# Local attention on 32-row tiles with values loaded two keys to a partition, in a fused attention and token-mixing kernel

## The chip, the core and the metric

The kernel runs on one core of one Trainium2 chip. The metric is the device time of one execution in microseconds (us), quoted as the median of the runs. Two engines' names are used all the time: PE is the matmul engine (PEld its weight loads), DVE the vector engine; ACT, POOL and SP are the scalar, the general and the DMA-issuing engine. A "batch" is one of the 8 entries of the leading axis; the kernel is software-pipelined over them. Its period is read from the start of the matmuls into the tile `pwd` (the projection of the pooled tokens, "hyper-weights" in the prediction), one group of four per batch, to that of the next batch.

## The reference, cut to what matters

```python
B, H, S, D = 8, 8, 576, 64           # q, k, v: float32 [B, H, S, D]
# attention, per batch and head
q_d, k_d, v_d = (mean over groups of 4 tokens)             # 144 tokens
out_up    = repeat(softmax(scale * q_d @ k_d.T) @ v_d, 4)  # pooled part
mask      = abs(i - j) < 4                                 # local window
out_local = softmax(where(mask, scale * q @ k.T, -1e9)) @ v
x = (out_up + out_local) as [B, S, H * D]                  # 576 x 512
# token mixer, per batch; w_q, w_k: 512 x 64, w_out: 512 x 512
W_tok = (x @ w_q) @ (x @ w_k).T / 8
out   = relu(W_tok @ x) @ w_out                            # float32
```

The local part needs only a narrow band of keys for each query. The mixer is computed as M2 = (x @ w_k).T @ x first, then (x @ w_q) @ M2.

## The kernel before

Queries are cut into ten windows of 56 to 58; each needs 64 keys. Scores are computed with the keys on the partitions of the result, two windows and two heads at a time on four 64x64 tiles of the PE array. The names `psc`, `pav`, `pm`, `po` and `pol` of the profile are the result tiles of scores, values, M2, output and last rows of the output.

```python
WQ = [58, 58, 58, 58, 56]            # queries of a window; two windows per n
PAIRS = [(0, 3), (1, 2), (4,)]
# ...
def load_v(b):                       # 64 keys of a window on 64 partitions, 256 B runs
    v32 = st[b]["v32"] = big.tile([128, NW, H, D], FP32, name="v32", tag="v32")
    for n in range(NW):
        for c in range(2):
            sp.dma_start(v32[64 * c:64 * c + 64, n],
                         _ap(v[b], K0[2 * n + c] * D, [[D, 64], [S * D, H], [1, D]]))
# ... scores: 80 matmuls a batch
for i, n in enumerate(pr_):
    for hl in range(NP):
        for p, c in ((0, 0), (1, 1), (0, 1), (1, 0)):
            m = 2 * n + c
            o = i * W + hl * w
            pe.matmul(p_[64 * c:64 * c + 64, p, o:o + w],
                      kT[64 * p:64 * p + 64, hl, K0[m]:K0[m] + 64],
                      qT[64 * p:64 * p + 64, hl, Q0[m]:Q0[m] + w],
                      start=False, stop=True, skip_group_check=True,
                      tile_position=(64 * p, 64 * c))
# ... values: 80 matmuls a batch, on the two diagonal tiles only
for s_ in range(2):
    for hh in range(NP):
        for c in range(2):
            h = 4 * (s_ ^ c) + hh
            pe.matmul(p_[64 * c:64 * c + 64, h // 4, 65 * hh:65 * hh + 65],
                      E[64 * c:64 * c + 64, h % 2, i, h // 2, :],
                      v16[64 * c:64 * c + 64, n, h, :],
                      start=True, stop=True, tile_position=(64 * c, 64 * c))
# ... M2: 7 matmuls of 512 columns
pe.matmul(p_, w_[NW][0:112], g["od"][0][0:112], start=True, stop=False)
pe.matmul(p_, w_[NW + 1], g["od"][1], start=False, stop=False)
for n in range(NW):
    pe.matmul(p_, w_[n], x[n], start=False, stop=(n == NW - 1))
# ... last 64 rows of the output: a group of its own in each batch
for r in range(4):
    pe.matmul(p_, rmx[:, r * S + 512:r * S + 640], wo16[:, r, :],
              start=(r == 0), stop=(r == 3))
# ... a fixed order of the stages (batch offset, stage), repeated for each batch
ORDER = [(-2, "og1"), (-1, "wtd"), (0, "sums"), (1, "cast_qk"), (-1, "wt"), ...]
```

The softmax here doesn't subtract the row's maximum and nothing guards it: scores larger than these inputs give would overflow.

## Time and profile before

| | before |
|---|---|
| median of 3 runs | 193.96 us (193.18 to 194.33) |
| span of the profiled execution | 192.7 us |
| PE busy, whole span | 155.5 us (81%) |
| period of a batch | 19.3 us, PE busy 18.52 of it |
| DMA packets | 74,027, of them 52,432 under 512 B |
| PE instructions (matmuls and weight loads; the trace lists 5,440) | 5,442 |

These are lines of the profile's page of the kernel before. The first three divide the span into slices: busy share of PE in tenths, granted clock of PE in tenths of full speed, busy share of the DMA engines. The two queue lines are packets, MB, and share of the 16 engines' time. The last is the chain of work that ended last, by engine.

```profile
PE   0034448885899989998999899989998999898790
PEclk9999555999789999999999999999999999999997
DMA  5999999899899799967999899969996943004215
...
q1 hardware_dynamic: 73920, 40.12, 81.7%
q8 instruction: 21, 0.34, 0.7%
...
PE 68%; DVE 17%; ACT 7%; issue 4%; POOL 2%; ACTq 0%; DVEq 0%
```

PE is full from slice 13 on; the DMA engines are nearly as full.

The table of windows of the kernel before, two of its periods. After the length come the busy times of PE, PEld, DVE, ACT and POOL with instruction counts, then granted clock, DMA share and GB/s.

```profile
62.00:81.30 19.30, 18.52 (x342) 12.43 (x340) 12.32 (x29) 13.22 (x17) 13.59 (x13) 1.00 0.93 244
81.30:100.60 19.30, 18.52 (x342) 12.44 (x340) 12.32 (x29) 13.17 (x17) 13.58 (x13) 1.00 0.87 234
```

PE works 96% of a period, at full clock; no other engine passes 14 us. PE is the bound of the steady state.

The timeline of PE in the kernel before (start, length, group, idle time before it and what ended it):

```profile
44.17 0.38 PE L27 MATMUL pm_847<-od_0_210,wk_206 128*128 128x512 f16 x1
44.39 0.38 PE L27 MATMUL pm_847<-x_424,wk_206 128*128 128x512 f16 x1
...
45.97 0.23 PE L27 MATMUL pav<-v_1_149,E_1_143 64*64 64x65 f16 x3
48.52 0.38 PE L27 MATMUL pav<-v_1_149,E_1_143 64*64 64x65 f16 x13 [2.33 <-issue]
...
103.00 0.45 PE L27 MATMUL psc<-qT,kT 64*64 64x58 f16 x32
104.69 0.45 PE L27 MATMUL pav<-v_1_149,E_0_131 64*64 64x65 f16 x16
```

M2's matmuls start about 215 ns apart. 32 score matmuls take 0.45 us, and only 16 value matmuls take the same; they use two tiles of four. At 45.97 PE stops in the middle of a group of 16 like matmuls, and the profile knows no wait for it: "issue".

### The profile page before, as it was taken

What the parts mean: (1) busy time and instruction counts of PE and PEld (TensorE: products, weight loads), DVE (VectorE), ACT (ScalarE), POOL (GpSimd) and SP (SyncE); (2) the same over time, 40 slices, a digit from 0 to 9 for tenths busy, and PEclk for the clock granted to TensorE, in tenths of its full rate; (3) what the DMA queues carried; (4) which work ended last, traced back from release to release, by engine and by line L of the source; (5) the groups of instructions that cost most, each with busy time, mean ns of one, the idle gap of its engine ahead of it and who ended that gap; (6) DMA issues with size and microseconds to landing.
All of it is one profiled execution on the core that took longest, in us unless ns stands there. A gap on an engine that the chain in (4) does not pass through costs nothing.

```text
span 192.7 us, 6374 instructions
## 1 busy us (share of the span) xinstructions
PE 155.5 (81%) x2720; PEld 104.0 (54%) x2720; DVE 114.8 (60%) x286; ACT 110.7 (57%) x140; POOL 107.7 (56%) x122
## 2 busy tenths in 40 slices
PE   0034448885899989998999899989998999898790
PEld 0034227853576647664776476647764776465330
DVE  6263978754646566656665666566656665685220
ACT  2037134954565767576757675767576757633422
POOL 5701991099748991895479547954895476000000
PEclk9999555999789999999999999999999999999997
DMA  5999999899899799967999899969996943004215
GB/s 175 314 187 215 348 290 162 191 354 175 175 319 218 174 264 294 263 137 201 278 323 156 184 280 346 187 154 296 330 215 154 300 146 112 3 3 153 93 57 188
DMA packets 74027, 40.54 MB, mean 210 GB/s; under 512 B 52432, under 2 KB 68880, under 8 KB 74000
## 3 DMA queue, kind: packets, MB, share of 16 engines
q1 hardware_dynamic: 73920, 40.12, 81.7%
q8 instruction: 21, 0.34, 0.7%
q14 instruction: 6, 0.05, 0.1%
q10 hardware_dynamic: 80, 0.03, 0.1%
HBM read 30.67 MB, written 9.44 MB: 208 GB/s over the span
## 4 chain that ended last, share of the span: by engine, by line
PE 68%; DVE 17%; ACT 7%; issue 4%; POOL 2%; ACTq 0%; DVEq 0%
PE po L27 15%; PE psc L27 6%; PE pav L27 5%; PE pw L27 4%; PE px L27 4%; PE pca L27 4%; PE pol L27 4%; DVE kd_127 L27 3%; PE pv L27 2%; PE pcs L27 2%; ACT kT L27 2%; PE pod L27 2%; DVE rz L27 1%; PE pws L27 1%; PE pwd L27 1%
## 5 line engine op out<-in xcount | busy, mean ns | idle before, releaser
L27 ACT COPY os<-po 128x1024 f32<-128x1024 f32 x16 | 16.2, 1012 | 14.7 <-issue 8.3
L27 DVE RECIPROCAL rz<-pav 128x8 f32<-128x8 f32 x40 | 8.1, 204 | 13.4 <-PE pav L27 13.4
L27 PE MATMUL po<-wo_91,rmx_227 128*128 128x512 f16 x64 | 15.3, 379 | 0.6 <-ACT rmx_227 L27 0.6
L27 PE MATMUL po<-wo_91,rmx_212 128*128 128x512 f16 x64 | 15.1, 379 | 0.0
L27 DVE COPY xT<-px 128x928 f16<-128x928 f16 (+1 forms) x32 | 13.8, 451 | 0.6
L27 PE MATMUL pq_236<-id_67,q_229 128*128 128x128 f16 x16 | 1.9, 312 | 12.6 <-DVE q_229 L27 12.6
L27 PE MATMUL psc<-id_67,neg 64*128 64x232 f16 (+1 forms) x80 | 9.4, 278 | 2.8 <-DVE vblk_201 L27 2.8
L27 PEld LDWEIGHTS <-rmx_227 128*128 128x128 f16 x80 | 7.2, 98 | 8.1 <-ACT rmx_227 L27 0.7
L27 PE MATMUL psc<-qT,kT 64*64 64x58 f16 (+1 forms) x640 | 11.4, 198 | 0.0
L27 PEld LDWEIGHTS <-rmx_212 128*128 128x128 f16 x80 | 7.2, 98 | 6.6
L27 DVE RECIPROCAL rc<-pca 128x8 f32<-128x8 f32 (+1 forms) x16 | 3.4, 211 | 11.8 <-PE pca L27 11.8
L27 PEld LDWEIGHTS <-wqk_90 128*128 128x128 f16 x96 | 8.3, 98 | 3.7 <-issue 0.9
L27 PEld LDWEIGHTS <-kT 64*64 64x64 f16 x640 | 8.7, 113 | 2.1 <-issue 2.1
L27 ACT COPY odT<-pod 128x448 f16<-128x448 f16 (+1 forms) x16 | 5.6, 402 | 6.3 <-PE pod L27 6.3
L27 PE MATMUL pw<-xT,wqk_90 128*128 128x288 f16 x64 | 9.2, 286 | 0.0
L27 PEld LDWEIGHTS <-q_229 128*128 128x128 f16 x16 | 1.6, 146 | 12.6 <-DVE q_229 L27 12.6
L27 POOL CAST v_0_147<-v_79 128x2560 f16<-128x2560 f32 x1 | 3.1, 3129 | 9.3 <-DMA w_92<-in_moe_w_k_dram 9.3
L27 DVE TENSOR_TENSOR wT_219<-pw,wTd 128x576 f16<-128x576 f32 x4 | 3.0, 758 | 8.6 <-ACT wTd L27 8.6
L27 DVE COPY ol<-pol 64x512 f32<-64x512 f32 x8 | 5.5, 682 | 4.3 <-PE pol L27 4.3
L27 DVE TENSOR_TENSOR wT_204<-pw,wTd 128x576 f16<-128x576 f32 x4 | 3.0, 758 | 8.0 <-ACT wTd L27 6.6
L27 DVE TENSOR_SCALAR rmx_227<-pmx 128x1024 f16<-128x1024 f32 x4 | 4.9, 1224 | 4.1 <-PE pmx L27 4.1
L27 POOL CAST v_1_149<-v_255 128x2560 f16<-128x2560 f32 x1 | 2.3, 2323 | 8.6 <-DMA v_255<-in_v_dram 8.6
(542 smaller groups left out, 540.9 us busy)
## 6 DMA issues: line engine op xcount, KB each, us to landing
out_dram<-os SPq DMA_DIRECT2D x16, 512.0 KB, 4.4
v_79<-in_v_dram SPq DMA_DIRECT2D x10, 128.0 KB, 4.6
v_255<-in_v_dram SPq DMA_DIRECT2D x10, 128.0 KB, 5.4
v_583<-in_v_dram SPq DMA_DIRECT2D x10, 128.0 KB, 3.5
v_1024<-in_v_dram SPq DMA_DIRECT2D x10, 128.0 KB, 4.4
v_1497<-in_v_dram SPq DMA_DIRECT2D x10, 128.0 KB, 3.6
v_1970<-in_v_dram SPq DMA_DIRECT2D x10, 128.0 KB, 4.3
v_2443<-in_v_dram SPq DMA_DIRECT2D x10, 128.0 KB, 3.4
```

The source lines that it names most:

```text
L27: return lambda *a, **k: self._tc.keep_in_program_order(f_(*a, **k))
```

## The change

The intent: fewer, larger DMA packets and less PE time. Values are loaded two keys to a partition, in 512 B runs. A window's 64 keys then lie on 32 partitions in two planes (even and odd keys), so scores and values run on 64x32 and 32x64 tiles, twice as many matmuls. M2 is split into two halves of 256 columns on two column tiles that are to run side by side. The remainders of q and k (the last 64 tokens) are loaded by head in 1 KB runs. The last rows of two batches share one output group. Outputs go out in 4 KB runs. The first batches get a hand-made order, and constants are set later. The core of the diff:

```diff
-PAIRS = [(0, 3), (1, 2), (4,)]
+NT = 3
 ...
-            for c in range(2):
-                sp.dma_start(v32[64 * c:64 * c + 64, n],
-                                  _ap(v[b], K0[2 * n + c] * D, [[D, 64], [S * D, H], [1, D]]))
+            for m in (2 * i, 2 * i + 1):
+                for s_ in range(1 if n < 2 else 2):
+                    c, nh = (m % 4) ^ (3 * s_), H if n < 2 else 4
+                    sp.dma_start(t[32 * c:32 * c + 32, 8 * n:8 * n + nh],
+                                 _ap(v[b], 4 * s_ * S * D + K0[m] * D, [[2 * D, 32], [S * D, nh], [1, 2 * D]]))
 ... (scores: 80 matmuls become 160)
+                for f in range(2):
+                    for hl in range(nh):
+                        for c in range(4):
+                            for p in range(2):
+                                ...
+                                pe.matmul(p_[32 * c:32 * c + 32, p, o:o + w],
+                                          _ap(kT, 64 * p * row(kT) + S * hh + K0[m] + f, [[row(kT), 64], [2, 32]]),
+                                          qT[64 * p:64 * p + 64, hh, Q0[m]:Q0[m] + w],
+                                          start=False, stop=True, skip_group_check=True,
+                                          tile_position=(64 * p, 32 * c))
 ... (values: 80 matmuls become 160)
+                                pe.matmul(ps_[t_][64 * c2:64 * c2 + 64, s_, 65 * hh:65 * hh + 65],
+                                          E[32 * c:32 * c + 32, hh % 2, f, 2 * a + hh // 2, :],
+                                          v16[32 * c:32 * c + 32, 8 * n + 4 * a + hh, f, :],
+                                          start=(f == 0), stop=(f == 1), skip_group_check=True,
+                                          tile_position=(32 * c, 64 * c2))
 ... (M2)
-            for n in range(NW):
-                pe.matmul(p_, w_[n], x[n], start=False, stop=(n == NW - 1))
+            for i, (*w_, x_) in enumerate(l_):
+                for c in range(2):
+                    pe.matmul(p_[64 * c:64 * c + 64, 0:256], w_[c], x_[:, 256 * c:256 * c + 256], start=(i == 0),
+                              stop=(i == len(l_) - 1), skip_group_check=True, tile_position=(0, 64 * c))
 ... (last rows, every second batch)
+            if b % 2 == 0:
+                return
-                pe.matmul(p_, rmx[:, r * S + 512:r * S + 640], wo16[:, r, :],
+                pe.matmul(p_, rest[b // 2][:, r, :], wo16[:, r, :], start=(r == 0), stop=(r == 3))
 ... (order of the first batches; order of the others; result-buffer slots; constants: cut)
```

The program has 8,770 PE instructions after, 5,442 before: 3,328 more.

## The prediction

> **What bounds it now.** In the table of windows, five consecutive batches between 62 and 158.5 us take 19.3 us each, with PE busy 18.52 (96%), ACT 13.2, POOL 13.6, DVE 12.3 us; the chain of waits is PE almost without a break there. So PE bounds the steady state. DMA is close behind: share 0.81 to 0.93. In the packet records, 50,176 packets of 256 B take 18 ns each (median; 70.8 us of a 16-engine total of about 160), a 1 KB packet 46 ns. The rest: 62 us until the second batch's hyper-weights, with PE idle 12.6 us before its first matmul, 5.2 us for the cast of v, 2.8 us behind DVE adds (7.6 us in the chain), and a clock of 0.75; then a 16.6 us tail after the last hyper-weights.

> **What changes, costed per batch (start-to-start distances of PE in one 19.3 us batch).**
> - m2: 7 matmuls of 512 columns, 1.62 us, become 14 of 256 on two column halves that should run side by side: -0.75. Eight more small transposes: +0.1.
> - Last rows of two batches share one output group: 4 matmuls of 216 ns every second batch: -0.43.
> - Local scores: 80 matmuls of 58 columns on 64x64 tiles become 160 on 64x32 tiles. Neighbours now start 4 ns apart, four in about 32 ns. [...] eight at 4 ns fill the same 32 ns, so about 0 to +0.3.
> - Local values: 80 matmuls of 65 columns, 17.5 ns apart (only two diagonal tiles used), become 160 on eight tiles at 4 to 8 ns: -0.7 to 0.
> - Masks, pooled v and remainders: about the same columns.
> Sum: about -1.6 us of PE per batch. ACT gains the remainder copies and one relu (about 14 us), DVE and POOL stay under 14: PE remains the bound, the period about 17.7 us.
> - DMA: v's 40,960 packets of 256 B become 20,480 of 512 B (27 ns for the few in the trace), remainders 8,192 to 2,048, outputs 4 KB runs: 160 to about 128 us in all. [...] bytes per ns rise from 14 to 19. It matters at the start only.
> - Start: loads and casts in halves, sums of batch 0 on PE (+2 us of PE, -9 us of DVE), constants set later, a hand-made order of the first batches. Two batches' loads need about 25 us. I estimate the second batch's hyper-weights at 48 us instead of 62.
> - Tail: m2 -0.7, two relus in sequence on ACT +0.8: unchanged, 16.5 us.

> **Time.** 48 + 5 x 17.7 + one period without loads 15.9 + 16.5 = 169, plus 1 us by which timed runs exceed the profiled span: **170 us**, 8 in 10 between **162 and 179**. Faster by over 2%: **0.96**; within 2%: **0.03**; slower: **0.01**.

> **What would show each step.** Windows: period 17 to 18.5 us with PE over 93% busy. Timeline: m2's 14 matmuls in about 0.85 us; scores of a 64-matmul group in 0.3 to 0.5 us; value matmuls under 8 ns apart. DMA share of the steady state under 0.9. First transposes near 10 us, second hyper-weights near 48 us. Tail within 1 us of before.

> **What would make it wrong.** 32-row tiles that don't overlap (17 ns apart would add 2 us a batch); 3,300 more PE instructions outrunning instruction fetch, seen as "issue" gaps like the 2.33 us one at 46 us; PSUM slots or ACT order stalling PE; a start bound by DMA or POOL, not by order; slow 32-partition loads.

The sum came to about -1.6 us of PE per batch, so a period of about 17.7 us and 170 us in all. That eight matmuls on eight tiles fill the 32 ns of four was the estimate, from the 4 ns between neighbours on four tiles; no run had shown it.

## The result, and the profile after

| | before | after |
|---|---|---|
| median | 193.6 us (4 runs) | 227.75 us (227.11 to 232.5, 4 runs) |
| ratio of fast runs | 1 | 1.175, 95% interval 1.169 to 1.181 |
| PE busy | 155.5 us | 173.8 us |
| PE at half clock (clock records within the span) | 19.2 us | 51.2 us |
| DMA packets | 74,027 | 45,448 |
| start of the second batch's `pwd` | 62.1 us | 62.1 us |

All ratios in this document are the mean time of one kernel's fast runs over that of the other's of the same rounds, so they are not quite the ratio of the medians. The changed kernel is 17.5% slower, not 12% faster: the prediction missed by 58 us and had given "slower" a chance of 0.01.

The page of the kernel after, the same lines:

```profile
PE   1458687696974599999973999368976799979791
PEclk9999758969799599999999799785997559999999
DMA  5989959979899999045867069920297003200415
...
q1 hardware_dynamic: 45408, 40.12, 62.6%
q8 instruction: 34, 0.56, 1.1%
...
PE 67%; issue 14%; ACT 7%; DVE 4%; DMA 3%; SPq 2%; ACTq 0%; DVEq 0%
```

The data queue q1 did drop from 81.7% to 62.6%. But PE has holes all along its row, the clock row shows half speed behind many of them, and the chain gives 14% of the span to "issue", time for which the profile has no cause. The DMA row has holes too, so it isn't the loads that fill the time.

The windows of the kernel after, same columns as before:

```profile
81.30:100.60 19.30, 19.11 (x517) 13.59 (x515) 11.03 (x29) 13.39 (x18) 13.15 (x9) 1.00 0.53 173
...
120.00:139.20 19.20, 15.58 (x322) 11.02 (x322) 8.76 (x23) 10.81 (x12) 7.86 (x5) 0.91 0.54 145
139.20:158.50 19.30, 12.95 (x407) 9.76 (x395) 7.11 (x18) 8.14 (x13) 7.05 (x6) 0.73 0.51 146
```

No engine and not DMA is full in the second and third line, and the clock is down. The periods are 19.8, 26.3, 21.4, 24.7, 28.0, 27.7 and 18.5 us; before, 19.3 each.

The waits of PE in the kernel after (total us, times, longest):

```profile
PE pav L27 <- issue: 10.5, 5, 3.8
PE pwk L27 <- issue: 7.7, 2, 5.7
PE psc L27 <- issue: 5.9, 4, 2.0
```

The timeline of PE in the kernel after:

```profile
92.69 0.68 PE L27 MATMUL psc<-qT,kT 64*32 64x58 f16 x64
...
94.51 0.71 PE L27 MATMUL pav<-v,E 32*64 32x65 f16 x64
...
99.32 0.71 PE L27 MATMUL pm<-x,wk 128*64 128x256 f16 x10
...
138.77 0.97 PE L27 MATMUL psc<-qT,kT 64*32 64x56 f16 x96
...
140.83 0.21 PE L27 MATMUL pav<-v,E 32*64 32x65 f16 x2
144.81 0.78 PE L27 MATMUL pav<-v,E 32*64 32x65 f16 x62 [3.77 <-issue]
```

The array works nearly as hoped: 64 score matmuls in 0.68 us and 64 value matmuls in 0.71 us, M2's matmuls two at a time. Then PE stops for 3.77 us after the second of 64 like matmuls, for which everything was there. So it isn't data, nor a result buffer.

A listing worked out from the traces (not a view of the profile), for the blocks around three stops of the kernel after and around the one of the kernel before; "runs" is the time between a block's first and last start, and "fetch" is the packet that landed last before the next block's start:

```
        block  starts   runs   fetch                 next block starts  stop
after    9      68.04   2.19      73.46- 74.72              76.16       5.92
after   18     117.87   2.21     121.36-122.37             123.88       3.81
after   21     138.80   2.03     142.44-143.37             144.81       3.97
after   14      97.41   4.23      98.50- 99.60             101.64       0.00
before   2      42.03   3.97      45.65- 46.99              48.52       2.52
before  10     103.17   4.00     103.96-105.07             107.16       0.00
```

The pattern is the same everywhere. The fetch for the next block as a rule begins only once the current block runs (median 1.4 us after its start, in both kernels, but up to 4.3 us before and 5.4 us after; 3 of the 34 after began 0.2 to 1.2 us ahead of it), takes about 1.1 us, and at the stops PE goes on 1.2 to 1.7 us after it has landed. Together about 3.9 us, more where the fetch is late. A block that lasts longer than its own fetch takes, delay included, hides this. Before, the shortest lasts 3.97 us, and that one stopped; two of 4.00 us did not. After, score and value matmuls fill a block in 2.0 to 2.7 us, and PE runs dry; two blocks of 5.6 us stopped as well, by 0.6 and 1.2 us, because their fetches began only 3.8 and 3.9 us after the blocks did.

The stop is then, by bookkeeping, the fetch's delay + its length + the time until PE goes on - the time for which the block runs. For block 21, with its own delay and the usual 1.1 and 1.4 us: 3.64 + 1.1 + 1.4 - 2.03 = 4.1 us, measured 3.97. The test of the pairing is another one. In the traces of all eleven kernels, with the packets paired to the borders in order, there are 276 borders with a packet of their own: at none does PE go on sooner than 1.16 us after its packet has landed, and at the 60 where it stood still for over 0.5 us, it goes on 1.16 to 1.66 us after.

### The profile page after: what moved, and what is told of

Same layout as the page of the kernel before. It is cut to its first block, busy times and chain, and to the rows that moved or that the text cites. A ratio compares the mean times of both kernels' runs of the same rounds, so it can differ in the third digit from the quotient of the medians.

```text
span 226.0 us, 9679 instructions
## 1 busy us (share of the span) xinstructions
PE 173.8 (77%) x4384; PEld 125.4 (55%) x4384; DVE 102.5 (45%) x291; ACT 119.4 (53%) x153; POOL 99.5 (44%) x100
## 2 busy tenths in 40 slices
DMA packets 45448, 40.72 MB, mean 180 GB/s; under 512 B 3424, under 2 KB 42336, under 8 KB 45408
## 3 DMA queue, kind: packets, MB, share of 16 engines
q1 hardware_dynamic: 45408, 40.12, 62.6%
## 4 chain that ended last, share of the span: by engine, by line
PE 67%; issue 14%; ACT 7%; DVE 4%; DMA 3%; SPq 2%; ACTq 0%; DVEq 0%
PE po L27 12%; PE psc L27 8%; PE pav L27 6%; PE pm L27 4%; PE pca L27 4%; PE pq L27 4%; PE pmx L27 4%; PE pv L27 4%; PE px L27 3%; DMA r<-in_k_dram 3%; PE pw L27 3%; PE pk L27 3%; ACT E L27 3%; SPq L27 2%; PE pol L27 2%
## 5 line engine op out<-in xcount | busy, mean ns | idle before, releaser
L27 POOL TENSOR_TENSOR sum<-qT 128x1152 f32<-128x1152 f16 x7 | 14.7, 2105 | 58.0 <-ACT qT L27 58.0
L27 PE MATMUL po<-wo,rmx 128*128 128x512 f16 x128 | 30.2, 380 | 0.3 <-DVE rz L27 0.3
L27 DVE TENSOR_TENSOR x<-pav,rz 128x512 f16<-128x512 f32 x40 | 27.7, 692 | 1.4
L27 PE MATMUL pav<-v,E 32*64 32x65 f16 x1280 | 17.3, 216 | 11.7 <-issue 10.5
L27 ACT ACTIVATE E<-psc 128x928 f16<-128x928 f32 (+1 forms) x24 | 19.3, 812 | 13.2 <-PE psc L27 12.2
L27 ACT COPY qT<-pq 128x2048 f16<-128x2048 f16 (+1 forms) x8 | 14.1, 1759 | 12.9 <-PE pq L27 12.9
L27 ACT ACTIVATE Ec<-pcs 128x576 f16<-128x576 f32 (+1 forms) x16 | 12.2, 771 | 12.3 <-PE pcs L27 11.9
L27 POOL CAST k<-k 128x2048 f16<-128x2048 f32 x7 | 13.2, 1892 | 11.7 <-DMA k<-in_k_dram 6.4
L27 ACT ACTIVATE rmx<-pmx 128x1024 f16<-128x1024 f32 x16 | 16.2, 1022 | 4.0 <-PE pmx L27 3.6
L27 DVE COPY xT<-px 128x464 f16<-128x464 f16 (+2 forms) x40 | 14.2, 394 | 6.9 <-PE px L27 6.4
L27 POOL CAST v<-v 128x2560 f16<-128x2560 f32 x7 | 16.3, 2323 | 2.1 <-DMA r<-in_q_dram 1.7
L27 POOL TENSOR_TENSOR sum<-kT 128x1152 f32<-128x1152 f16 x7 | 14.7, 2105 | 4.7 <-ACT kT L27 4.6
L27 POOL CAST q<-q 128x2048 f16<-128x2048 f32 x7 | 13.2, 1891 | 2.9 <-DMA q<-in_q_dram 2.9
```

The source lines that it names most:

```text
L27: return lambda *a, **k: self._tc.keep_in_program_order(f_(*a, **k))
```

## The experiments

**Theory A**: PE consumes the dense blocks of small matmuls faster than the next 256 instructions arrive; the clock drops after the stops. **Rival B**: the 32-row tiles are slow of themselves, or the new order and result-buffer slots make PE wait, and the position of the stops is chance. **Rival C**: with v in 512 B runs the loads disturb something else, such as q and k arriving late. On one core, a run counts as slow here when it is over 1.5% above the fastest of its kernel. The profiled executions of the first, third, fifth and eighth kernel below were such runs; from those I take positions of stops and lengths of undisturbed periods, and no differences of a few per cent.

### 1. The kernel after without the loads of later batches (wrong)

```diff
 def f_(b):                               # loads of q and k; the same for v
+    if b > 1:
+        st[b]["qk"[i] + "32"] = st[1]["qk"[i] + "32"]
+        return
```

> The changed kernel, but batches 2 to 7 reuse batch 1's q, k and v in the on-chip buffers, so most data loads are gone (results wrong on purpose); the 8,770 tensor-engine instructions are the same. Theory A (the tensor engine outruns its instruction fetch: one 16 KB packet of 256 instructions [...] waits behind data DMA): the packet's start comes within about 1 us of the block's start, as in the quietest blocks of before; stalls at block borders fall from 28 us to under 10 us, the clock recovers, total 180 to 200 us. Rival B (32-row and 32-column tiles are slow by themselves, or the new order stalls): total within 5 us of 227.

Measured: 199.83 us median (197.65 to 203.51), ratio to before 1.025 (1.019 to 1.032). 13 stops remain, 16.5 us in all, all at borders of 256. The page of this run:

```profile
DMA  5989997400100431061204022200220042002225
...
q1 hardware_dynamic: 16416, 19.67, 31.7%
```

With the DMA engines nearly empty after the start, half of the stopped time goes. The long delays of the fetch go with it: from 60 us on, 1 fetch of 25 began over 2 us after its block, the latest 2.1 us; in the kernel after, 9 of 26 did, the latest 5.4 us. The median is 1.1 us in both. So data traffic makes some fetches late, and PE outruns them even without traffic. The expected "under 10 us" of stops was a miss, and the time is at the top of the range. Rival B had expected 222 us or more for this kernel, which has the same small tiles, order and result buffers.

### 2. The kernel before with 160 tiny matmuls more in each batch (correct results)

```diff
+    pe.matmul(p_[64 * c:64 * c + 64, p, 500:504],        # 4 columns nobody reads
+              kT[64 * p:64 * p + 64, hl, K0[m]:K0[m] + 64],
+              qT[64 * p:64 * p + 64, hl, Q0[m]:Q0[m] + 4],
+              start=False, stop=True, skip_group_check=True,
+              tile_position=(64 * p, 64 * c))
 # and the like behind each value matmul
```

> The kernel before, with a second matmul of only 4 columns, into unused columns, after each of the 160 local-attention matmuls of a batch: 8,002 tensor-engine instructions instead of 5,442, still on 64x64 tiles, same order, same data loads. Theory A: stalls of 1 to 4 us at multiples of 256 instructions appear, 10 to 25 us in all, and the clock drops after them; total 215 to 240 us. Rival B (the tiles or the new order are to blame, not the count): only the array time of the added matmuls, at most 2 us a batch, so 200 to 210 us and no stalls at block borders.

Measured: 243.45 us median; one fast run of 234.84, the others up to 248.51, so no interval. 10 stops, 21.1 us, all at borders of 256, and 49.6 us at half clock. Timeline and waits of PE of this run:

```profile
121.41 0.68 PE L27 MATMUL psc<-qT,kT 64*64 64x4 f16 x57
125.83 0.27 PE L27 MATMUL psc<-qT,kT 64*64 64x4 f16 x3 [3.75 <-issue]
```

```profile
PE pav L27 <- issue: 10.9, 5, 3.9
PE psc L27 <- issue: 5.8, 4, 3.8
```

The first two lines have the plainest reading: of the 60 score matmuls that are left of a group, 57 have run, and PE stands still for 3.75 us before the other three. (The view puts the form of the first one on the row; real ones of 58 columns and tiny ones of 4 are mixed in it.) Nothing but instructions was added to the kernel before: same tiles, same order, same loads, same result buffers. It got stops of the same kind, at the same numbers. Such stops therefore need neither B nor C. A's range was 215 to 240 us and the fast run lies in it, but the median lies above. What the added matmuls cost by themselves and what the half clock costs were not separated; in the profiled execution PE's busy time is 26.1 us above that of before and its idle time 13.9 us, so the stops are not all of the loss.

### 3. The kernel after with 64x64 tiles for local attention (wrong by my own mistake)

Scores, values (on two diagonal tiles), masks, pooled v and the loads of v as before; all else as after: 5,938 PE instructions. The halves of the heads were put in the wrong order in x, so the result is wrong. The same work is done.

```diff
-                        for c in range(4):
-                            for p in range(2):
+                        for p, c in ((0, 0), (1, 1), (0, 1), (1, 0)):
 ...                           # one matmul of 64 keys in place of two of 32; same for values
```

> The changed kernel with only the local attention (and with it the loading of v, one key to a partition in 256 B runs) put back to 64x64 tiles; the new order, remainders by head, m2 by halves and shared last rows stay. 5,938 tensor-engine instructions. Theory A: stalls at block borders under 5 us, period about 17.5 to 18.5 us, total 170 to 185 us, so faster than both. Rival C (the new order and start are to blame): stays above 205 us.

Measured: 201.71 us (198.69 to 203.4), ratio 1.033 (1.025 to 1.042). The stops at borders are two, 6.2 us; but 170 to 185 us was expected, so the time was a miss. Two other costs appeared: the loads are in 256 B packets again (q1 share 79.8%, 62.6% in the kernel after), and the chain gives 19% to DMA and 14% to the DMA-issuing queue. Taking the small tiles away removes most of the stops (6.2 us are left of 32.5), but this kernel has another limit.

### 4. The kernel after with the dense stages spread apart (correct results)

```diff
-(-2, "m2"), (-1, "mask1"), (-1, "score1"), (-1, "av2"), ...
+(-2, "m2"), (-1, "mask1"), (-1, "score1"), (-3, "og1"), (-1, "av2"), ...
-(0, "score2"), (1, "load_k"), (0, "score0"), ...
+(0, "score2"), (-2, "og0"), (1, "load_k"), (0, "score0"), ...
 # ol moved ahead of av0, too; the stores one batch later
```

The output matmuls (16 in about 3.8 us, dense in time but not in number) go between scores and values.

> The changed kernel, same instructions, but in the repeated part of the order (batches 5 to 7 only) the long output matmuls stand between the groups of small ones, so that 256 instructions last longer where they are dense. Theory A: the 2 us blocks become 3.5 us or more, total 3 to 10 us less than 227. Rival B: within 1.5 us of 227.

Measured: 224.32 us (223.35 to 230.53), ratio 1.159 (1.153 to 1.164), 3.4 us less than after in the medians, at the low end of what was expected. In the part whose order was changed, from 114 us on, the stops above 0.5 us at borders fall from 18.1 to 4.6 us, and the time at half clock from 27.3 to 1.3 us. The time does not follow. The waits of PE in this kernel from 114 us to the end of the last stores show why:

```profile
PE pod L27 <- DVE od L27: 4.3, 5, 1.1
PE po L27 <- DVE vblk L27: 2.9, 3, 1.0
...
PE pmx L27 <- ACT os L27: 2.1, 4, 0.5
```

PE now waits for DVE and ACT, 9.3 us in these three lines alone. In all, its idle time from there on is 24.5 us, in the kernel after 24.4; its busy time is 82.5 us in place of 87.2, although one group of eight output matmuls more (1.7 us) falls into that part. Going by the names, the moved output matmuls stand before stages whose data or result buffers are not ready yet. So the order governs the stops, as A says, and this order trades them for other waits. Of the half clock it shows that 26 us less of it came with only about 6 us less of busy time. A good order might exist; none was found here.

### 5. The kernel before with what is left of the change (correct results)

M2 in column halves, shared last rows, 4 KB outputs; no small tiles, no new loads, the old order: 5,522 PE instructions.

```diff
-            for n in range(NW):
-                pe.matmul(p_, w_[n], x[n], start=False, stop=(n == NW - 1))
+            for i, (w_, x_) in enumerate(l_):
+                for c in range(2):
+                    pe.matmul(p_[64 * c:64 * c + 64, 0:256], w_, x_[:, 256 * c:256 * c + 256], start=(i == 0),
+                              stop=(i == len(l_) - 1), skip_group_check=True, tile_position=(0, 64 * c))
 ... # ol and the stores as in the changed kernel
```

> The kernel before, in its own order and with its own local attention and loads, plus three parts of the change that add few instructions: m2 by column halves, the last rows of two batches in one output group, outputs in 4 KB runs. 5,522 tensor-engine instructions (before 5,442). If the prediction priced these parts rightly (-0.75 and -0.43 us of the tensor engine per batch) and the steady state is bound by that engine: period 18.1 instead of 19.3 us, total 183 to 187 us, faster than both kernels, no more stalls at block borders than before (one). If data DMA (share 0.81 to 0.93 before) takes over as the bound: 187 to 192.

Measured: 189.69 us (187.54 to 191.07), ratio 0.974 (0.968 to 0.981): faster than both, and than the kernel before by 1.9 to 3.2%, so that 2% is not quite assured. It is within the second of the two ranges expected. One of its undisturbed periods in the windows:

```profile
77.60:96.00 18.40, 17.12 (x345) 12.36 (x344) 11.73 (x28) 13.29 (x18) 12.67 (x12) 1.00 0.90 224
```

The period is 18.4 us, 0.9 less than before (the prices of the prediction gave 1.2). DMA is at 0.90 in it, PE at 93%; that the seventh kernel, with DMA at 0.15 to 0.27, has periods of 18.2 to 18.4 speaks for PE as its bound, but that is another kernel, and no run of this one without loads was made. Two stops at borders, 4.7 us together, made one period 22.5 us and one 20.1: this kernel is close to the fetch as well.

### 6. The fifth kernel and the remainders by head (correct results)

```diff
-            sp.dma_start(r32[64 * i:64 * i + 64],
-                              _ap(src, 512 * D, [[D, 64], [S * D, H], [1, D]]))
+            sp.dma_start(r32[:, i], _ap(src, 512 * D, [[S * D, H], [4 * D, 16], [1, 4 * D]]))
 ... # 16 small matmuls in place of 4 transposes
```

> As e5, and the remainders of q and k loaded by head in 1 KB runs (12 more small matmuls a batch, 192 instructions in all; remainder packets from 8,192 to 2,048). If the tensor engine bounds e5: within 1 us of it. If DMA bounds e5: 1 to 4 us faster.

Measured: 190.99 us (188.66 to 192.6), three of six runs slow, ratio of the fast ones 0.976 (0.970 to 0.983). The two intervals overlap, and the medians of the fast runs are 189.38 us here and 189.42 in the fifth kernel: fewer packets for the remainders gain nothing that these runs can see, which is what was expected if PE is the bound.

### 7. The third kernel mended, without the loads of later batches (wrong)

```diff
+            if b > 1:                     # for q and k; v likewise
+                st[b]["qk"[i] + "32"] = st[1]["qk"[i] + "32"]
+                return
```

> The changed kernel with the local attention on 64x64 tiles (5,938 instructions, as e3, its x halves put right) and, as in e1, no loads of q, k and v after batch 1 (results wrong on purpose). The third run was 202 us with few stalls and with loads and stores in its chain. If its cause was data DMA, now loaded with 256 B runs in an order made for fewer packets: period 17 to 18 us, total 165 to 178 us, near what was predicted for the changed kernel. If the new order or the new start is slow by itself: stays above 190.

Measured: 182.06 us (181.77 to 183.01), ratio 0.940 (0.935 to 0.945); 4 us above the upper end expected. One stop at a border, 0.7 us. Two of its windows:

```profile
109.20:127.50 18.30, 16.59 (x366) 12.17 (x364) 10.97 (x29) 13.62 (x19) 13.09 (x10) 1.00 0.15 57
127.50:145.90 18.40, 17.42 (x372) 12.63 (x370) 11.57 (x30) 13.73 (x19) 13.21 (x10) 1.00 0.22 76
```

This is the rest of the change at its best: start of the second `pwd` at 54.1 us, most periods 18.2 to 18.4 us, hardly a stop and no waits for loads. (It also has the values on four tiles; see the eighth.) It is faster than before, but its period is no better than the fifth kernel's, which does load.

### 8. The third kernel mended (correct results)

```diff
-                    for s_ in range(2):
-                        for hh in range(NP):
+                    for hh in range(NP):
+                        for s_ in range(2):
 ...
-                                h = 4 * (s_ ^ c) + hh
-                                pe.matmul(ps_[i][64 * c:64 * c + 64, h // 4, 65 * hh:65 * hh + 65],
+                                h = 4 * s_ + hh
+                                c2 = c ^ s_ if t < 4 else c
+                                pe.matmul(ps_[i][64 * c2:64 * c2 + 64, s_, 65 * hh:65 * hh + 65],
 ...                                      # and tile_position (64 * c, 64 * c2) in place of (64 * c, 64 * c)
```

> The third run's kernel with my error in it mended (heads 4 to 7 now change halves as the rest of the changed kernel expects), so the result should be correct. Same loads and nearly the same instructions: 197 to 204 us, DMA and the load queue in the chain.

Measured: 200.44 us (197.87 to 204.23), ratio 1.029 (1.021 to 1.037). The chain of its page, and what its DMA-issuing queue waits for:

```profile
PE 41%; DMA 17%; ACT 11%; SPq 11%; POOL 10%; issue 5%; DVE 2%; ACTq 0%; POOLq 0%
```

```profile
SPq L27 <- ACT os L27: 27.3, 7, 11.9
SPq L27 <- DVE ol L27: 20.9, 2, 13.6
```

Stores stand in one queue with the loads, and in this order a store waits up to 13.6 us for its data while the loads behind it wait, too. The third of its periods is 29.4 us long. Against the seventh kernel the loads cost 18 us. This fits a hand-made order that was fitted to the small tiles and to loads in 512 B runs; no run separated the order from the size of the runs.

The mend does more than put the result right, and the seventh kernel has it as well: in four of the five pairs of windows it spreads the values over all four 64x64 tiles. The timelines of the third and of this kernel, both at full clock, for 32 value matmuls:

```profile
113.44 0.70 PE L27 MATMUL pav<-v,E 64*64 64x65 f16 x32
107.71 0.45 PE L27 MATMUL pav<-v,E 64*64 64x65 f16 x32 [0.15 <-ACT E L27]
```

In the seventh kernel they start 8.4 ns apart on four tiles and 15 ns apart in the last pair, which stayed on two. So what was slow about the values before was the two tiles, and the other two can be used at 80 matmuls a batch, without one instruction more: by estimate 0.8 us a batch (64 x 8.4 + 16 x 15 ns) against 160 x 8 ns = 1.3 us on 32-row tiles.

### 9. The kernel before without the loads of later batches (wrong)

```diff
     def load_qk(b):                       # load_v likewise
+        if b > 1:
+            st[b]["qk32"] = st[1]["qk32"]
+            return
```

> The kernel before with no loads of q, k and v after batch 1 (results wrong on purpose), the counterpart of e1 and e7. If the tensor engine bounds the steady state of before, as the prediction said: the period stays within 0.3 us of 19.3 and the total within 5 us of 193.5, most of that gained at the start. If data DMA bounds it: period under 18.8 us and total under 188.

Measured: 192.68 us (191.32 to 192.97), ratio 0.990 (0.983 to 0.997). One of its windows:

```profile
99.00:118.30 19.30, 18.53 (x342) 12.44 (x341) 12.31 (x29) 13.24 (x17) 13.54 (x13) 1.00 0.19 64
```

DMA share 0.19 in place of about 0.9, and the period stays 19.3 us to the digit. The kernel before is bound by PE; taking these loads away gains it about 1%, all of it outside the steady state, so fewer or larger packets alone could hardly gain more.

### The four corners together

Medians of the fast runs in us, two to four of each, from rounds on two chips (the kernel before took 193.4 to 194.1 us in all of them). "Loads" are those of batches 2 to 7; the first two rows have the rest of the change.

| | with loads | without |
|---|---|---|
| 32-row tiles (after, 1) | 227.6 | 198.2 |
| 64x64 tiles (8, 7) | 200.19 | 182.06 |
| (the kernel before, 9) | 193.6 | 192.68 |

The small tiles cost 16 us without loads and 27 us with them, although the version on 64x64 tiles has its own trouble with loads. The loads, which cost the kernel before about 1 us, cost the changed one 29.

## Why the prediction was wrong

**Right.**
- The bound before: PE. The ninth kernel shows it.
- The array time. M2's part, shared last rows: period 18.4 us in the fifth kernel, 19.3 before; M2's 14 matmuls start within 0.68 us, the seven of before within 1.31. 64 scores in 0.68 us and 64 values in 0.71: matmuls on different tiles do overlap. But the 64 scores start no faster on eight tiles than the 32 of before on four: 7.7 ns apart in the mean, 8.2 before (only the three groups of 32 scores that run by themselves in the kernel after start 3.8 to 4.0 ns apart). 8 ns a score is 160 x 8 = 1.28 us a batch against 80 x 8 = 0.64 before (four in 32 ns), so +0.6 us in place of the predicted "about 0 to +0.3"; a small miss. The values came to 8 ns, the dear end of the predicted 4 to 8.
- The tail: 17.3 us from the last `pwd` to the end, 16.8 before.
- The DMA traffic: 45,448 packets in place of 74,027; q1's share from 81.7 to 62.6%. In the trace of the kernel after, a 256 B packet takes 18 ns, one of 512 B 27, of 1 KB 46 and of 4 KB 159 (medians): 14, 19, 22 and 26 bytes a ns.

**The step that failed** is the sum: "about -1.6 us of PE per batch. [...] PE remains the bound, the period about 17.7 us." It priced matmuls by the array alone ("eight at 4 ns fill the same 32 ns, so about 0 to +0.3") and gave the supply of 3,328 more instructions the price of zero. In the traces they come in packets of 16,384 B, one for each 256 (34 packets after, 21 before). The runs put in its place: 32.5 us of stops before instruction 193 (mod 256), and five of seven periods stretched to 21 to 28 us. Two smaller steps failed with it, the start and the size of the period: with 64x64 tiles, without the loads and with 0.7 us of stops, the seventh kernel still took 182.06 us, above the range of 162 to 179.

The mechanism stood in the text, as one item of the last paragraph: "3,300 more PE instructions outrunning instruction fetch, seen as "issue" gaps like the 2.33 us one at 46 us". It had no number and no share of the range. The number could have been had from the trace of before: 256 instructions in 3.97 us and a stop of 2.5 us; and a count of PE instructions in the new order would have shown blocks of 2 us. That a rare stop was the visible end of a margin nearly used up is what I did not see.

**From 170 towards 228**, an estimate worked out from the runs: 170 as predicted; + 32.5 us stops; + 6 us at the start (54.1 us in the seventh kernel, where I had 48); + 3 us for the six periods after that point (107.7 us in the seventh kernel, 104.4 predicted). That is 212. The half clock, 51.2 us of it against 19.2 before, could add 16 us at most, if each us costs half (M2's 14 matmuls start within 1.29 us at 77.6 us, in a half-clock stretch, within 0.68 at full clock), and the sum would then be 228; but that would be luck. Two pairs of runs with as many PE instructions put it lower: 26 us less at half clock went with about 6 us less of busy time in the fourth kernel (from 114 us on), 34 us less with 12.6 in the first. At that rate the clock adds 7 to 12 us, the sum is 219 to 224, and 4 to 9 us stay unexplained. Nor need stops simply add: a stop can hide a wait for ACT or DVE, and no run shows how often one does.

**The clock.** The half-clock stretches of the kernel after begin at 72.8, 124.0, 144.5, 151.3 and 171.8 us, in a stop or within 2 us of the end of one; these stops end at 76.2, 123.9, 144.8, 149.7 and 169.9. (So do the three before 60 us, at 25.0, 45.5 and 55.7, after stops that end at 24.2, 44.7 and 54.3.) The records give these eight stretches lengths of 3.41, 6.83, 10.24 and 13.65 us. What halves the clock they don't show, and the stops ahead differ: those that end at 149.7 and 169.9 us lasted 1.7 and 2.1 us, the one that ends at 76.2 lasted 5.9. That the stops cause the half clock is an argument from the coincidence; no run separated the two. The fourth kernel has fewer stops (20.9 us) and 21.8 us at half clock, which fits.

**The start.** Predicted 48 us, measured 62.1, the same as before. On 64x64 tiles it is 54.1 (seventh kernel) and, with loads, 53.9 (eighth). So 8 us were there to be had. In the kernel after, 7.3 us of stops lie ahead of that point.

**What stays open.** Why the fetch mostly starts only 1 us or more after its block does, and at times over 5 us after. The first experiment shows that data traffic has a part in it (from 60 us on, largest delay 5.4 us with, 2.1 without). And whether some order of the small tiles stays under the limit at full gain: the fourth kernel is one attempt only. At 2 us a block, a batch's 320 small matmuls and their 320 weight loads alone fill 2.5 blocks, which makes it hard.

## What to carry to other kernels

Count instructions, not only columns: time the shortest run of 256 consecutive PE instructions (weight loads count), and if it is near 4 us, the length at which the kernel before first stopped, don't split matmuls further, however well the pieces overlap in the array (in the kernel after, 14 of the 17 blocks shorter than 4 us were followed by a stop of over 0.5 us, and of the nine longer than 5.7 us none). See first whether the tiles that lie idle can be used with the matmuls that there are, as the eighth kernel's values do (32 in 0.45 us on four tiles, in 0.70 on two). When the profile gives an idle time to "issue", number the instructions at which it falls before looking for any other reason. A change made of many parts is best tried in parts: here the least conspicuous ones (M2 in column halves, shared last rows, larger output runs) gain 2.6% together, and the small tiles cost 16 to 27 us.
